# An attention and MLP kernel on one core: a new order of the same instructions, four stores for eight, and 64 products of zeros

## The chip, the cores and the metric

The kernel runs on one core of one Trainium2 chip. The metric is the device time of one execution in microseconds (us); the time of a kernel is the median of its runs. The engines are TensorE (PE, with PEld for its weight loads), VectorE (DVE), ScalarE (ACT), GpSimd (POOL) and SyncE (SP), which issues nearly all DMA.

## The reference

```python
kv = np.einsum('bhsd,bhse->bhde', k, v)            # 8 batches, 8 heads, 576 tokens, 64 wide
out = np.einsum('bhsd,bhde->bhse', q, kv)
out = out / np.sqrt(np.mean(out * out, axis=-1, keepdims=True) + 1e-6) * g_norm
x = out.transpose(0, 2, 1, 3).reshape(4608, 512)
h = x @ w_in                                       # 512 x 2048
return ((h * np.cos(h)) @ w_out).astype(np.float32)   # 2048 x 512
```

The weights arrive as 64-bit floats; everything is held to float32 accuracy.

## The kernel before

**Accuracy.** TensorE multiplies in a reduced float format (fp32r), so each operand is split into a high part and a low rest (`xhi`/`xlo`, `ghi`/`glo`, and the two halves of a weight tile), and each product is three: high by high, low by high, high by low. An operand costs a copy on ACT (the high part) and a subtraction on DVE or POOL (the rest).

**Chunks and steps.** The 4608 tokens are 9 chunks of 512. Chunks 0, 1 and 2 are worked plainly: a step is one tile of 128 hidden columns, `stage1_part` (12 products of 128x512 into a `bank`), `act_part` (h·cos h on ACT and DVE) and `stage2_part` (12 products into the four `acc` banks). The order is chunk 0 with tiles 0 to 3, chunk 1 with tiles 0 to 7, chunk 0 with 4 to 15, chunk 1 with 8 to 15, chunk 2. Between its two stretches chunk 0's sums are stored aside (`part0_0` to `part0_3`), and loaded again into a `slot` tile when they are completed (`out_part`). Chunks 3 to 8 are worked two at a time by a scheme with seven products in place of eight (`quad_part`), which needs sums and differences of w_in's tiles. `sums_part` makes them on POOL and stores them in DRAM (`wq`), from where they come back (`load_in`).

**The front.** Until the first step can run, k, v and q of the first two batches are loaded, `kv_front_part` and `x_front_part` make x for chunks 0 and 1, and `w_part` turns each raw weight tile into float32 and its two halves: on DVE a `TENSOR_SCALAR` on the low words (or the same on ACT), two `SCALAR_TENSOR_TENSOR` and one `TENSOR_TENSOR`, which writes the low half. 32 weight tiles pass through it in the first 130 us. The tiles are named `wi0` to `wi15` (w_in) and `wo0` to `wo15` (w_out); `m`, `sg`, `slot`, `r`, `ki` are shared working tiles.

**What sets the order.** Every engine works through its own queue in program order. That order is fixed when the kernel is built, by a planner in the kernel itself, class `Order`: each part asks for an engine and a time ("run"), waits for events or takes a token of a pool of buffers, and the planner hands the engines out by planned start and priority. The priorities are due times (`due`) plus a number for each part from the table `haste` (`put_off`); `gate` moves a part's earliest start by the same table. A DMA is planned as a time on SP, a time on the DMA engines and a delay until it counts as landed:

```python
    DMA_LAT = 1.6
    ...
    def flight(us, done):
        _, end = yield "run", [("DMA", us)], -1e3
        sched.give(t_fly, end + DMA_LAT)
        sched.fire(done, end + DMA_LAT)
```

The numbers decide nothing but the order: on the chip each instruction starts when its inputs and buffers are there. At the very start 40 products of zeros of 128x128 run on TensorE before the first data are in.

Of the kernel before, what the change touches and what calls it, by code (L numbers as in the profile page):

```python
# [10 lines left out]
F32 = mybir.dt.float32  # L11
# [174 lines left out]
def tile_kernel(  # L186
# [133 lines left out]
    def due(i):  # L320
# [7 lines left out]
        ('acc', 0): -308.36, ('acc', 1): 50.25, ('acc', 10): -89.24, ('acc', 11): -14.97, ('acc', 12): 244.72,  # L328
        ('acc', 13): -313.02, ('acc', 14): 115.67, ('acc', 15): -2.01, ('acc', 16): 9.58, ('acc', 17): -346.93,
        ('acc', 18): -115.97, ('acc', 19): 1122.67, ('acc', 2): 3.24, ('acc', 20): 388.25, ('acc', 21): 12.32,  # L330
        ('acc', 22): 45.65, ('acc', 23): 116.02, ('acc', 24): 93.39, ('acc', 25): -81.12, ('acc', 26): 284.61,
        ('acc', 27): 173.19, ('acc', 28): 102.47, ('acc', 29): 272.34, ('acc', 3): 49.44, ('acc', 30): -435.3,
        ('acc', 31): -431.32, ('acc', 32): -992.81, ('acc', 33): 118.14, ('acc', 34): 910.79,
        ('acc', 35): -309.89, ('acc', 36): 59.17, ('acc', 37): -20.74, ('acc', 38): -32.87, ('acc', 39): -11.87,
        ('acc', 4): -30.22, ('acc', 40): 329.51, ('acc', 41): 625.48, ('acc', 42): 79.92, ('acc', 43): 86.88,
        ('acc', 44): -161.65, ('acc', 45): 53.41, ('acc', 46): -145.28, ('acc', 47): 11.24, ('acc', 5): 244.28,
        ('acc', 7): 38.42, ('acc', 8): -20.95, ('acc', 9): -331.3, ('act', 0): -1.32, ('act', 1): -0.36,
        ('act', 10): 47.7, ('act', 11): -521.03, ('act', 12): -6.85, ('act', 13): -404.2, ('act', 14): -28.25,
        ('act', 15): -476.92, ('act', 16): 108.57, ('act', 17): -5.46, ('act', 18): -111.25, ('act', 19): 31.06,
        ('act', 2): 111.53, ('act', 20): 273.1, ('act', 21): -100.42, ('act', 22): -27.84, ('act', 23): -116.33,  # L340
        ('act', 24): -81.98, ('act', 25): -7.56, ('act', 26): -5.19, ('act', 27): -29.04, ('act', 28): 65.34,
        ('act', 29): -38.82, ('act', 3): 0.76, ('act', 30): -52.43, ('act', 31): 380.56, ('act', 32): 70.27,
        ('act', 34): -48.89, ('act', 35): 445.1, ('act', 36): -27.7, ('act', 37): -6.52, ('act', 38): 103.18,
        ('act', 39): -38.48, ('act', 4): -60.27, ('act', 40): 1650.37, ('act', 41): 104.72, ('act', 42): 179.73,
        ('act', 43): -0.49, ('act', 44): -9.15, ('act', 45): 28.81, ('act', 46): -152.26, ('act', 5): -0.59,
        ('act', 6): 50.53, ('act', 7): -7.88, ('act', 8): -0.49, ('act', 9): -221.89, ('cross', 0, 1): 14.87,
        ('cross', 1, 0): 270.69, ('cross', 1, 1): 237.31, ('cross', 2, 0): -223.42, ('cross', 2, 1): -397.6,
        ('gate keep in', 0): -313.88, ('gate keep in', 1): 77.44, ('gate keep in', 10): -411.52,
        ('gate keep in', 11): 38.86, ('gate keep in', 12): -993.27, ('gate keep in', 13): -979.61,
        ('gate keep in', 14): -141.94, ('gate keep in', 15): -16.43, ('gate keep in', 3): -727.27,  # L350
        ('gate keep in', 4): -1000.22, ('gate keep in', 5): 0.65, ('gate keep in', 6): -937.07,
        ('gate keep in', 7): 0.69, ('gate keep in', 8): 3.68, ('gate keep in', 9): -4.83,
        ('gate keep out', 0): 64.24, ('gate keep out', 1): 94.89, ('gate keep out', 10): -7.93,
        ('gate keep out', 11): -813.7, ('gate keep out', 12): -28.32, ('gate keep out', 13): -310.7,
        ('gate keep out', 14): -193.87, ('gate keep out', 15): -131.44, ('gate keep out', 2): 1.29,
        ('gate keep out', 3): 7.99, ('gate keep out', 5): -25.65, ('gate keep out', 6): -76.31,
        ('gate keep out', 7): 11.3, ('gate keep out', 8): 6.07, ('gate keep out', 9): 14.4,
        ('gate kv', 2): -119.99, ('gate kv', 3): 8.42, ('gate kv', 4): -89.12, ('gate kv', 5): -201.39,
        ('gate kv', 7): -260.05, ('gate load', 2): -1.73, ('gate load', 3): -19.79, ('gate load', 4): -246.31,
        ('gate load', 5): 23.96, ('gate load', 6): 1.63, ('gate load', 7): -70.84, ('gate sums', 0): -0.29,  # L360
        ('gate sums', 1): -1.99, ('gate sums', 2): 99.41, ('gate sums', 3): -10.12, ('gate sums', 4): -10.76,
        ('gate sums', 5): -175.34, ('gate sums', 6): 18.29, ('gate sums', 7): -6.45, ('gate x', 2, 0): -118.84,
# [153 lines left out]
    kv_tiles, q_tiles, xs, w_raw, w_split = {}, {}, {}, {}, {}  # L516


    DMA_LAT = 1.6

    t_fly = Tokens(8)

# [17 lines left out]
    def copies(out, in_, us):  # L540
        return us, lambda: sp.dma_start(out=out, in_=in_)
# [1191 lines left out]
```

## Time and profile before

| | |
|---|---|
| median of 3 runs | 843.74 us (841.93 to 843.87) |
| the profiled execution's own time | 844.5 us |
| its span, first to last instruction | 842.6 us |
| PE busy | 823.7 us, 98% of the span |
| DVE busy | 614.8 us, 73% |
| ACT busy | 501.8 us, 60% |
| POOL busy | 233.1 us, 28% |
| mean granted TensorE clock | 0.996 of full speed |

The busy time of PE holds its waits only where they are longer than the tail of the product before; its idle time is what is left of the span. A busy share over the whole span says little of the first 125 us, in which DVE is as full as PE.

### The profile page before, as it was taken

Reading aid. Unit: us, or ns where it says so; the run is one execution under the profiler, and the core shown is the slowest. Engines: PE = TensorE matmul, PEld = TensorE weight load, DVE = VectorE, ACT = ScalarE, POOL = GpSimd, SP = SyncE. Lnnn points to the kernel's source line nnn. Section 1 sums busy time; section 2 is a strip of 40 time slices with the busy share of each in tenths; the row PEclk is TensorE's granted clock in tenths of the full one; section 3 lists DMA queues with packets and bytes.
Section 4 is the critical chain, followed back from the end, with each engine's and each line's share of the span. In section 5 each row is a group of like instructions: output and inputs, shape, how many; then the busy total and the mean of one; then the engine's idle time right before and its main releaser. Section 6 shows DMA issues by size and latency. Waiting matters only on the chain.

```text
span 842.6 us, 12666 instructions
## 1 busy us (share of the span) xinstructions
PE 823.7 (98%) x4376; PEld 679.6 (81%) x4376; DVE 614.8 (73%) x949; ACT 501.8 (60%) x984; POOL 233.1 (28%) x154
## 2 busy tenths in 40 slices
PE   7899999999999999999999999999999999999998
PEld 6678878887888788887888888888888888888886
DVE  2999996566778888879889988898666774535221
ACT  4888964544455567768658756676555653535321
POOL 3220067542326783104226512305214000000000
PEclk9899999999999999999999999999999999999999
DMA  9997526698463588897966776677757676663664
GB/s 310 302 387 288 181 70 222 202 288 263 120 195 100 134 261 251 229 321 204 287 201 197 219 208 202 186 217 234 201 182 244 179 212 205 202 226 100 226 205 144
DMA packets 150912, 181.21 MB, mean 215 GB/s; under 512 B 74432, under 2 KB 114112, under 8 KB 150848
## 3 DMA queue, kind: packets, MB, share of 16 engines
q1 hardware_dynamic: 150336, 179.68, 69.3%
q8 instruction: 35, 0.57, 0.3%
q10 hardware_dynamic: 512, 0.72, 0.2%
q14 instruction: 29, 0.24, 0.1%
HBM read 143.66 MB, written 36.70 MB: 214 GB/s over the span
## 4 chain that ended last, share of the span: by engine, by line
PE 83%; DVE 7%; DMA 4%; ACT 2%; issue 2%; SPq 1%; POOL 0%; DVEq 0%; ACTq 0%; POOLq 0%
PE acc L239 43%; PE bank L239 40%; DVE sg L239 2%; SPq L239 1%; DVE r L239 1%; DMA wi<-in_moe_w_in_dram 1%; DVE wi L239 1%; DMA sg<-in_v_dram 1%; DMA wi<-in_q_dram 1%; DVE glo L239 0%; DVE xlo L239 0%; DVE slot L239 0%; DMA qb<-in_q_dram 0%; DMA out_dram<-slot 0%; DVE qT L239 0%
## 5 line engine op out<-in xcount | busy, mean ns | idle before, releaser
L239 PE MATMUL acc<-wo,ghi 128*128 128x512 f32 x1152 | 356.6, 390 | 0.9 <-DVE slot L239 0.6
L239 PEld LDWEIGHTS acc<-wo,ghi 128*128 128x128 f32 x1152 | 214.9, 188 | 46.3 <-DVE slot L239 1.3
L239 PE MATMUL bank<-wi,wo 128*128 128x512 f32 (+2 forms) x1092 | 241.5, 379 | 1.2 <-DVE wi L239 1.0
L239 PEld LDWEIGHTS bank<-wi,wo 128*128 128x128 f32 (+2 forms) x1092 | 191.3, 185 | 42.5 <-DVE wi L239 2.5
L239 PE MATMUL acc<-wo,glo 128*128 128x512 f32 x576 | 224.4, 390 | 0.0
L239 POOL TENSOR_TENSOR rinv<-ms,mhalf 128x16 f32<-128x16 f32 (+1 forms) x36 | 97.2, 2701 | 206.4 <-DVE ms L239 206.3
L239 PEld LDWEIGHTS acc<-wo,glo 128*128 128x128 f32 x576 | 108.1, 188 | 22.6
L239 PE MATMUL bank<-xhi,wi 128*128 128x512 f32 x320 | 99.9, 393 | 1.4 <-DVE slot L239 1.1
L239 DVE TENSOR_TENSOR wi<-bank,wi 128x512 f32<-128x512 f32 x72 | 49.5, 688 | 44.1 <-PE bank L239 35.4
L239 DVE TENSOR_TENSOR glo<-wo,ghi 128x512 fp32r<-128x512 f32 x59 | 42.8, 726 | 42.6 <-ACT ghi L239 42.4
L239 PEld LDWEIGHTS bank<-xhi,wi 128*128 128x128 f32 x320 | 59.2, 188 | 14.3 <-issue 1.5
L239 ACT ACTIVATE ki<-wi 128x512 int32<-128x512 f32 x72 | 45.1, 627 | 37.2 <-DVE wi L239 28.8
L239 ACT CAST ghi<-wo 128x512 fp32r<-128x512 f32 x61 | 37.8, 620 | 46.4 <-PE acc L239 45.8
L239 ACT ACTIVATE ki<-bank 128x512 int32<-128x512 f32 x72 | 42.7, 593 | 34.2 <-PE bank L239 29.0
L239 PE MATMUL bank<-xlo,wi 128*128 128x512 f32 x160 | 62.4, 390 | 0.0
L239 ACT COPY wi<-bank 128x512 f32<-128x512 f32 x72 | 41.9, 584 | 30.7 <-PE bank L239 30.0
L239 DVE TENSOR_TENSOR glo<-r,ghi 128x512 fp32r<-128x512 f32 x60 | 46.5, 777 | 11.5 <-ACT ghi L239 10.9
L239 ACT ACTIVATE r<-r 128x512 f32<-128x512 f32 x60 | 37.9, 631 | 22.3 <-DVE r L239 22.0
L239 DVE SCALAR_TENSOR_TENSOR r<-bank,ki 128x512 f32<-128x512 f32 x51 | 34.9, 685 | 21.8 <-ACT ki L239 21.6
L239 ACT ACTIVATE wo<-wo 128x512 f32<-128x512 f32 x61 | 38.2, 629 | 21.3 <-DVE wo L239 20.9
L239 ACT CAST ghi<-r 128x512 fp32r<-128x512 f32 x60 | 37.2, 621 | 22.3 <-PE acc L239 16.9
L239 DVE TENSOR_TENSOR r<-r,bank 128x512 f32<-128x512 f32 x51 | 34.7, 681 | 4.6 <-ACT r L239 3.9
(171 smaller groups left out, 1074.9 us busy)
## 6 DMA issues: line engine op xcount, KB each, us to landing
wo<-wod SPq DMA_DIRECT2D x96, 512.0 KB, 4.1
wo<-wq SPq DMA_DIRECT2D x84, 512.0 KB, 4.2
out_dram<-slot SPq DMA_DIRECT2D x35, 256.0 KB, 3.7
wi<-in_moe_w_in_dram SPq DMA_DIRECT2D x16, 512.0 KB, 8.9
wo<-in_moe_w_out_dram SPq DMA_DIRECT2D x16, 512.0 KB, 9.4
wod<-wo SPq DMA_DIRECT2D x16, 512.0 KB, 4.7
wq<-wi SPq DMA_DIRECT2D x24, 256.0 KB, 3.6
m<-in_k_dram SPq DMA_DIRECT2D x24, 256.0 KB, 4.8
```

What stands on the lines that cost most here:

```text
L239: return lambda *a, **kw: tc.keep_in_program_order(f(*a, **kw))
```

## The change

1. The table `haste` is replaced as a whole, and with it the order on every engine.
2. The planner's costs change: 0.5 for 0.4 us of SP for each DMA, a landing delay of 1.3 us for loads and 0.7 for stores in place of 1.6 for both, and other times for some DMAs and ACT copies.
3. `sums_part` makes the differences in another order and into another tile, so that two results that lie in regular steps in `wq` stand side by side. Each is stored by one DMA of 256 KB where two of 128 KB stood: 4 stores for 8 in each of 8 calls, 32 DMAs fewer in all.
4. A new part, `warm_part(16)`, gives TensorE 16 times 4 products of zeros of 128x128, into the bank of `acc2`, at the lowest priority, after x of chunk 0's first part is done.

```diff
-    DMA_LAT = 1.6
+    DMA_LAT, STORE_LAT = 1.3, 0.7
...
-            yield "run", [("SP", 0.4)], prio
+            yield "run", [("SP", 0.5)], prio
...
+    def warm_part(n):
+
+        yield "wait", [x_done[0, 0]]
+        yield "take", t_acc[2], 1e6
+        spare = ps_o.tile([P, DM], F32, name="acc2")
+        for _ in range(n):
+            _, end = yield "run", [("PE", 0.22)], 1e6
+            for _ in range(4):
+                pe.matmul(out=spare[:, 0:P], lhsT=zeros, rhs=zeros, start=True, stop=True)
+        sched.give(t_acc[2], end)
...
-        for t, places in ((even, (S1, A22)), (odd, (S3, S2))):
-            slot = yield "take", t_slot, prio
+        for t, places in ((rest, (S2, S3)), (even, (S1, A22))):
+            slot = spare if t is rest else (yield "take", t_slot, prio)
...
             sched.spawn(sums_store(slot, [stored], prio + 20.0, [
-                copies(wq[:, 7 * m + q, n], part[:, half * WH:(half + 1) * WH], 0.35)
-                for half, q in enumerate(places) for n, part in enumerate((hi.bitcast(F32), t))]))
+                stores(
+                    wq[:, first:last + 1:last - first, n, :], part.rearrange("p (h f) -> p h f", h=2), 0.68)
+                for n, part in enumerate((hi.bitcast(F32), t))]))
...
-        ('acc', 0): -308.36, ('acc', 1): 50.25, ('acc', 10): -89.24, ('acc', 11): -14.97, ('acc', 12): 244.72,
+        ('acc', 0): -572.9, ('acc', 1): 26.2, ('acc', 10): 92.3, ('acc', 11): -57.9, ('acc', 12): 191.2,
```

What the new table does shows in the order of the built programs. Counted over the whole program each engine has nearly the same instructions as before: PE 64 products more (the zeros), DVE 6 small copies more and 6 additions fewer, POOL 6 additions more, SP 32 DMAs fewer.

**TensorE in the front.** The place is that of chunk 0's x: `acc<-ident,r` turns x of one part back (a part's last product), `bank<-...64x64` is a `kv_front_part`. Before:

```order
L239 MATMUL bank_362<-wo_173,wi_172 64x64 x12
L239 MATMUL bank_383<-wo_171,wi_170 64x64 x18
L239 MATMUL acc_339<-ident,r_420 128x128 x4
L239 MATMUL acc_448<-wo_158,m_263 128x2x64 x4
L239 MATMUL bank_461<-ident,wi_174 128x128 x4
L239 MATMUL acc_352<-ident,r_467 128x128 x4
```

And with the change:

```order
L239 MATMUL bank_353<-wo_173,wi_172 64x64 x12
L239 MATMUL acc_240<-ident,r_301 128x128 x4
L239 MATMUL bank_388<-wo_171,wi_170 64x64 x18
L239 MATMUL bank_425<-ident,wi_174 128x128 x4
L239 MATMUL acc_330<-ident,r_414 128x128 x4
L239 LDWEIGHTS zeros
L239 MATMUL acc_424<-zeros 128x128
```

Twelve products of zeros follow here in a row; the other 52 stand in blocks of 4 to 24 between the front's products from here to the last x of chunk 0, and none behind that.

**VectorE ahead of w_out's tile 7.** The rows end with the one that writes the low half of `wo7`, which is the first operand of chunk 0's or 1's step 7 in stage 2. `sg`, `m` belong to `w_part`, `r`, `ki` and `bank` to `act_part`. Before:

```order
L239 TENSOR_TENSOR wo12_1493<-sg1_1396,wo12_1493 128x512
L239 TENSOR_TENSOR r1_1491<-r1_1491,bank3_1449 128x512
L239 TENSOR_SCALAR m1_1511<-wo15_864 128x512
L239 SCALAR_TENSOR_TENSOR sg2_1434<-wo7_332,sg2_1434 128x512
L239 SCALAR_TENSOR_TENSOR sg1_1509<-sg1_1509,m1_1511 128x512
L239 TENSOR_TENSOR wo7_1522<-sg2_1434,wo7_1522 128x512
```

And with the change:

```order
L239 TENSOR_TENSOR wo9_1579<-sg0_1487,wo9_1579 128x512
L239 SCALAR_TENSOR_TENSOR sg4_1539<-sg4_1539,m4_1556 128x512
L239 TENSOR_TENSOR r2_1585<-r2_1585,bank2_1535 128x512
L239 SCALAR_TENSOR_TENSOR r0_1611<-bank3_1566,ki_1603 128x512
L239 SCALAR_TENSOR_TENSOR sg4_1539<-wo7_323,sg4_1539 128x512
L239 TENSOR_TENSOR r0_1611<-r0_1611,bank3_1566 128x512
L239 TENSOR_TENSOR wo7_1624<-sg4_1539,wo7_1624 128x512
```

From DVE's first weight instruction (the `TENSOR_SCALAR` on the first weight tile's low words) to this row there were 172 instructions and are 180 (7 more of 128x512 with two tensors, 1 more `TENSOR_SCALAR` of 128x512). PE's first product with `wo7` had 345 products of 128x512 ahead of it and has 357. To the last `r<-bank,rinv` of chunk 1's x the same counts are 78 and 70 on DVE (7 and 1 fewer) and 90 and 69 on PE.

**SyncE where chunk 0's sums come back.** `slot<-part` loads the four sums again, `out_dram<-slot` stores the completed rows, `qb` loads q for chunk 2, `wod` and `wq` are stores of weights. Before:

```order
L239 DMA slot_2226<-part_1_1321_1045 128x512
L239 DMA qb_2183<-in_q_dram 32x4x32
L239 DMA slot_2229<-part_2_1359_1073 128x512
L239 DMA out_dram<-slot_2161 128x512
L239 DMA wod_142<-wo_739 128x1024
L239 DMA sg_2217<-in_v_dram 128x2x256
L239 DMA wq<-slot_2148 128x256
L239 DMA qb_2183<-in_q_dram 32x12x32
L239 DMA wod_152<-wo_1277 128x1024
L239 DMA wq<-sg_2015 128x256
```

The first sum's load stands 12 rows above these, the fourth's 5 rows below. With the change:

```order
L239 DMA slot_2191<-part_0_1341_1120 128x512
L239 DMA qb_2180<-in_q_dram 32x4x32
L239 DMA slot_2199<-part_1_1355_1128 128x512
L239 DMA qb_2180<-in_q_dram 32x12x32
L239 DMA qb_2222<-in_q_dram 32x4x32
L239 DMA qb_2180<-in_q_dram 32x12x32
L239 DMA qb_2222<-in_q_dram 32x4x32
L239 DMA qb_2180<-in_q_dram 32x12x32
L239 DMA qb_2222<-in_q_dram 32x4x32
L239 DMA qb_2180<-in_q_dram 32x12x32
```

The third sum's load comes 2 rows further on, the fourth's 6: the four stand within 16 rows, where they stood within 27, and no store of weights is between them.

## Rows read from the trace of the kernel before

**Rows 1.** The page: its first line of busy times (us, share, instructions), and of the 40 slices (21 us each) the rows of PE, DVE and the granted clock, in tenths.

```profile
PE 823.7 (98%) x4376; PEld 679.6 (81%) x4376; DVE 614.8 (73%) x949; ACT 501.8 (60%) x984; POOL 233.1 (28%) x154
...
PE   7899999999999999999999999999999999999998
...
DVE  2999996566778888879889988898666774535221
...
PEclk9899999999999999999999999999999999999999
```

**Rows 2.** Busy time in stretches: from:to, length, busy us and instructions of PE, PEld, DVE, ACT and POOL, then the granted clock, the DMA engines' share and GB/s.

```profile
18.00:24.00 6.00, 3.38 (x68) 2.65 (x67) 5.41 (x12) 4.98 (x13) 3.28 (x2) 1.00 1.09 355
24.00:31.00 7.00, 6.08 (x46) 5.11 (x48) 6.02 (x11) 4.87 (x11) 1.64 (x1) 0.52 1.11 259
...
60.00:110.00 50.00, 49.38 (x222) 40.97 (x223) 49.85 (x85) 44.38 (x81) 2.21 (x2) 1.00 0.64 226
110.00:123.00 13.00, 12.70 (x57) 10.21 (x56) 12.85 (x18) 6.38 (x12) 11.39 (x6) 1.00 0.27 81
...
180.00:205.00 25.00, 22.81 (x103) 18.19 (x102) 16.68 (x26) 10.41 (x21) 5.58 (x3) 1.00 0.89 253
205.00:400.00 195.00, 193.12 (x1081) 159.67 (x1080) 164.37 (x255) 122.39 (x256) 80.94 (x51) 1.00 0.71 203
400.00:839.00 439.00, 438.71 (x2076) 362.39 (x2074) 294.03 (x446) 246.22 (x468) 80.13 (x42) 1.00 0.66 203
```

**Rows 3.** The timeline of PE in the front: start, length, engine, line, operation, output and inputs, count, and in brackets the idle time before it and what ended it.

```profile
0.98 3.75 PE L239 MATMUL bank<-zeros 128*128 128x128 bf16 x40 [0.98 <-DVE zeros L239]
...
22.29 0.63 PE L239 MATMUL acc<-ident,r 128*128 128x128 f32 x4 [2.03 <-DVE r L239]
23.19 0.49 PE L239 MATMUL acc<-wo,m 128*128 128x128 f32 x2 [0.28 <-ACT wo L239]
24.92 1.65 PE L239 MATMUL acc<-wo,m 128*128 128x128 f32 x6 [1.24 <-ACT wo L239]
```

**Rows 4.** Single microseconds of the same kind as rows 2, where the granted clock falls and where it is back.

```profile
24.00:25.00 1.00, 0.08 (x1) 0.08 (x1) 1.00 (x2) 0.94 (x4) 0.00 (x0) 0.66 1.10 266
...
30.00:31.00 1.00, 1.00 (x15) 0.78 (x15) 1.00 (x2) 0.52 (x2) 0.22 (x1) 0.50 1.18 259
31.00:32.00 1.00, 0.84 (x20) 0.70 (x17) 1.00 (x3) 0.97 (x4) 0.00 (x0) 0.93 1.07 368
```

**Rows 5.** The timeline of DVE and PE: DVE's first weight instruction, its two waits while PE ran at half clock, the last `r` of chunk 1's x and PE's product behind it.

```profile
18.88 0.43 DVE L239 TENSOR_SCALAR m<-wi 128x512 int32<-128x512 uint32 x1 [0.20 <-DMA wi<-in_moe_w_in_dram]
...
27.24 0.69 DVE L239 TENSOR_REDUCE ms<-slot 128x8 f32<-128x512 f32 x1 [0.81 <-ACT slot L239]
...
32.78 0.69 DVE L239 TENSOR_TENSOR wi<-sg,wi 128x512 fp32r<-128x512 f32 x1 [0.45 <-ACT wi L239]
...
62.94 0.68 DVE L239 TENSOR_TENSOR r<-bank,rinv 128x512 f32<-128x512 f32 x1
...
63.87 0.60 PE L239 MATMUL bank<-ident,r 128*128 128x128 f32 x4
```

**Rows 6.** The timeline of POOL, DVE and PE around `wo7`: POOL's first sum, DVE's instructions beside it, and PE's wait.

```profile
109.74 5.51 POOL L239 TENSOR_TENSOR m<-wi 128x512 f32<-128x512 f32 x1 [47.10 <-DVE sg L239]
...
115.57 1.67 DVE L239 SCALAR_TENSOR_TENSOR sg<-wo,sg 128x512 int32<-128x512 int32 x1
...
119.80 1.22 DVE L239 SCALAR_TENSOR_TENSOR sg<-wo,sg 128x512 int32<-128x512 int32 x1
120.95 1.23 DVE L239 SCALAR_TENSOR_TENSOR sg<-sg,m 128x512 int32<-128x512 int32 x1
122.10 0.68 DVE L239 TENSOR_TENSOR wo<-sg,wo 128x512 fp32r<-128x512 f32 x1
...
122.83 0.50 PE L239 MATMUL acc<-wo,ghi 128*128 128x512 f32 x1 [0.30 <-DVE wo L239]
```

**Rows 7.** The timeline of SP's queue (SPq), DVE and PE where chunk 0's sums come back.

```profile
193.04 0.38 SPq L239 DMA_DIRECT2D slot<-part  x1
...
193.96 0.46 SPq L239 DMA_DIRECT2D slot<-part  x1
...
197.32 0.69 DVE L239 SCALAR_TENSOR_TENSOR slot<-acc,slot 128x512 f32<-128x512 f32 x1 [3.21 <-DMA out_dram<-slot]
...
198.07 0.73 PE L239 MATMUL acc<-wo,ghi 128*128 128x512 f32 x2 [0.59 <-DVE slot L239]
...
201.01 0.70 PE L239 MATMUL bank<-xhi,wi 128*128 128x512 f32 x2 [1.13 <-DVE slot L239]
```

**Rows 8.** PE's other waits between 123 and 400 us: what waited for what, us in total, times, the longest.

```profile
PE bank L239 <- DVE wi L239: 1.0, 1, 1.0
...
PE bank L239 <- DVE r L239: 0.5, 1, 0.5
PE bank L239 <- DVE sg L239: 0.5, 1, 0.5
```

**Rows 9.** The timeline of DVE: the instructions ahead of the first and the last of these waits.

```profile
182.91 1.79 DVE L239 TENSOR_TENSOR sg<-qT,m 128x512 fp32r<-128x512 f32 x1
...
389.42 1.75 DVE L239 SCALAR_TENSOR_TENSOR xhi<-wi,ki 128x512 f32<-128x512 f32 x1
```

**Rows 10.** The page's DMA issues: what was moved by which queue, how often, KB each, median us to landing.

```profile
wq<-slot SPq DMA_DIRECT2D x32, 128.0 KB, 2.6
...
wq<-sg SPq DMA_DIRECT2D x16, 128.0 KB, 2.8
```

**Rows 11.** A stretch in which PE does nothing but products of 128x512, columns as in rows 2.

```profile
600.00:700.00 100.00, 100.00 (x443) 82.76 (x442) 69.85 (x101) 57.29 (x104) 13.18 (x8) 1.00 0.66 204
```

More of the change, by code (lines that the diff above doesn't have):

```diff
@@ L333, in tile_kernel @@
[L333 to L337, printed above, removed]
@@ L354, in tile_kernel @@
[L354 to L359, printed above, removed]
@@ L516, in tile_kernel, with flight, copies, stores @@
     kv_tiles, q_tiles, xs, w_raw, w_split = {}, {}, {}, {}, {}
-    DMA_LAT = 1.6
+    DMA_LAT, STORE_LAT = 1.3, 0.7
     t_fly = Tokens(8)
-    def flight(us, done):
+    def flight(us, late, done):
         _, end = yield "run", [("DMA", us)], -1e3
-        sched.give(t_fly, end + DMA_LAT)
-        sched.fire(done, end + DMA_LAT)
+        sched.give(t_fly, end + late)
+        sched.fire(done, end + late)
     def dmas(pieces, prio):
         landed = []
-        for us, issue in pieces:
+        for us, late, issue in pieces:
             yield "take", t_fly, prio
-            yield "run", [("SP", 0.4)], prio
+            yield "run", [("SP", 0.5)], prio
             issue()
             landed.append(Event())
-            sched.spawn(flight(us, landed[-1]))
+            sched.spawn(flight(us, late, landed[-1]))
         yield "wait", landed
         return max(e.t for e in landed)
-    def copies(out, in_, us):
-        return us, lambda: sp.dma_start(out=out, in_=in_)
+    def copies(out, in_, us, late=DMA_LAT):
+        return us, late, lambda: sp.dma_start(out=out, in_=in_)
+    def stores(out, in_, us):
+        return copies(out, in_, us, STORE_LAT)
     def load(prio, event, pieces, wait=(), take=None, first=None):
@@ L655, in pieces @@
                 src = moe_w_out[j * P:(j + 1) * P, :].rearrange("p (c f) -> p c f", f=P)
-            return [copies(t, src, 1.4 if kind == "wi" else 1.3)]
+            return [copies(t, src, 1.5 if kind == "wi" else 1.4)]
         return pieces
@@ L696, in copies @@
         def copies(j):
-            e, end = yield "run", [("ACT", 0.3, 0.0), ("DVE", 0.3, 0.3)], prio
+            e, end = yield "run", [("ACT", 0.45, 0.0), ("DVE", 0.45, 0.3)], prio
             for r in heads:
@@ L984, in x_norm @@
         sched.give(t_qT, end)
-        yield "run", [("ACT", 0.6)], prio
+        yield "run", [("ACT", 0.87)], prio
         swp = small.tile([P, TB], F32, name="swp")
@@ L1006, in x_norm @@
             aside = tc.dram_tile([P, CH], F32, name=f"x{c}_{p}")
-            end = yield from dmas([copies(aside, x, 0.68)], prio)
+            end = yield from dmas([stores(aside, x, 0.66)], prio)
             sched.give(t_slot, end, held)
@@ L1010, in x_norm @@
             x = store_tile(held)
-            end = yield from dmas([copies(x, aside, 0.68)], due(begin[PLAIN - 1]) + p)
+            end = yield from dmas([copies(x, aside, 0.9)], due(begin[PLAIN - 1]) + p)
         if c >= PLAIN:
@@ L1225, in out_part @@
         if before is not None:
-            yield from dmas([copies(o, before, 0.68)], prio)
+            yield from dmas([copies(o, before, 0.85)], prio)
             _, end = yield "run", [("DVE", dve_us(DM))], prio
@@ L1238, in out_part @@
             to = partial[c, t] = tc.dram_tile([P, DM], F32, name=f"part{c}_{t}_{sched.seq}")
-        end = yield from dmas([copies(to, o, 0.68)], prio)
+        end = yield from dmas([stores(to, o, 0.68)], prio)
         sched.give(t_slot, end, slot)
@@ L1281, in keep_in @@
         end = yield from dmas([
-            copies(wq[:, 7 * m + q], w[:, :, half * WH:(half + 1) * WH].bitcast(F32), 0.68)
+            stores(wq[:, 7 * m + q], w[:, :, half * WH:(half + 1) * WH].bitcast(F32), 0.68)
             for q, half in (((A11, 0), (A12, 1)) if j % 2 == 0 else ((S4, 1),))], prio)
@@ L1287, in keep_out @@
         yield "wait", [w_done["wo", j]]
-        end = yield from dmas([copies(wod[j], w_split["wo", j].bitcast(F32), 1.3)], prio)
+        end = yield from dmas([stores(wod[j], w_split["wo", j].bitcast(F32), 1.3)], prio)
         sched.fire(wo_kept[j], end)
@@ L1310, in sums_part @@
         pool.tensor_tensor(out=even, in0=odd, in1=even, op=ALU.subtract)
-        for out, a, b in (
-            (odd[:, low], odd[:, high], odd[:, low]),
-            (odd[:, high], odd[:, high], even[:, low]),
-            (even[:, high], even[:, low], even[:, high]),
-        ):
+        yield "run", [("POOL*", pool_us(WH))], prio
+        pool.tensor_tensor(out=even[:, high], in0=even[:, low], in1=even[:, high], op=ALU.subtract)
+        spare = yield "take", t_slot, prio
+        rest = slot_tile(spare)
+        for out, a, b in ((rest[:, low], odd[:, high], even[:, low]), (rest[:, high], odd[:, high], odd[:, low])):
             yield "run", [("POOL*", pool_us(WH))], prio
@@ L1318, in sums_part @@
         kept = []
-        for t, places in ((even, (S1, A22)), (odd, (S3, S2))):
-            slot = yield "take", t_slot, prio
+        for t, places in ((rest, (S2, S3)), (even, (S1, A22))):
+            slot = spare if t is rest else (yield "take", t_slot, prio)
             yield "run", [("ACT", act_us())], prio
-            hi = at.tile([P, CH], F32R, name=f"slot{slot}", bufs=1)
+            if t is rest:
+                hi = two(pair, [P, CH], F32R, 1)
+            else:
+                hi = at.tile([P, CH], F32R, name=f"slot{slot}", bufs=1)
             act.copy(out=hi, in_=t)
```

181 lines of the change are left out of this document (94 added, 87 removed), and 90 rows, old and new, of the table haste.

## The prediction

> **What bounds the kernel now.** I read the page's busy shares first. PE is busy 98% of the span, and 9 tenths or more in nearly every slice [rows 1]; the products themselves stay what they are, so only PE's waits and its slow stretch can be won. Next the stretches [rows 2]: behind 400 us PE has 0.3 us of idle time in 439, so nothing is to be had there, and the 3.7 us between the last product and the end of the span are the last stores. What is left lies in three places.
>
> First the front. From 18 us on DVE is as full as PE: 49.85 of 50 us between 60 and 110, 85 instructions, so 0.59 us from one to the next. PE has no such queue of its own making: it waits for `r`, the `wi` and the `wo` that DVE writes. The last such wait is 0.30 us, at 122.83 us, for the low half of `wo7`, which DVE wrote from 122.10 to 122.78 [rows 6]. So up to 123 us the end is set by DVE's queue: when DVE reaches `wo7`, and how much of PE's work is done by then. Second the clock: it falls to 0.5, the lower of its two levels (1.2 GHz), in the microsecond after 24 and is back in the one after 31 [rows 4]. Before it fell PE had waited 2.03, 0.28 and 1.24 us with little between [rows 3]. From 24.92 to 31 PE is busy at half speed, so it does about 3 us less than it could. But that is worth on the path only what DVE loses by it: DVE waits 0.81 and 0.45 us there for ACT's copies of what PE delivers late [rows 5]. Third five waits between 123 and 400 us: 0.59 and 1.13 us where chunk 0's sums come back [rows 7], and 1.0, 0.5 and 0.5 us elsewhere [rows 8].
>
> **The change, part by part.**
>
> *The zeros.* 64 more products. The 40 at the start take 3.75 us, 0.094 each [rows 3], so 64 cost PE 6.0 us at most, and nothing where they fill a wait. They stand among the products of 20 to 35 us, where PE waits for DVE and where 2.03 and 1.24 us of waits were; behind the last x of chunk 0 there are none. I charge nothing on the path, because DVE's queue sets the end there; if PE were the later one, the cost would be up to 6.0 less the waits that they fill. What they can give is the clock. If it holds, DVE's two waits shrink: −0.9 us of the 1.26, bounds 0 and −1.3. The Trainium skill, page "TensorE: Matmul & The Clock Gate", section "HAM oscillation — how this bites in real kernels", says that it is the long idle gaps between bursts that send the array back to half clock; the trace agrees in kind, but here the longest gap was 2.03 us. By that rule a filler that leaves such gaps changes nothing, and the −0.9 would be 0.
>
> *DVE's queue to `wo7`.* From the first weight instruction (18.88 us [rows 5]) to `wo7` there were 172 instructions and are 180. Seven more with two tensors at 0.59 and one short one at about 0.35 (its 0.43 less the overlap): +4.5 us. The start: the first weight tile is now the 13th of SP's loads and was the 14th; one load of v of 0.29 MB less at 355 GB/s [rows 2] is −0.8 us (0 to −0.9). The waits of DVE: −0.9, from above. POOL: its first sum starts at 109.74, and DVE's instructions beside it take 1.67, 1.22 and 1.23 us in place of the 0.68 of `wo7`'s own row [rows 6], 2.1 us more together; and DVE's 18 instructions from 110 to 123 us fill 12.85 us [rows 2], where 18 at 0.59 fill 10.6: about 2.2 us are lost beside POOL. In the new order POOL's first sum writes a tile that DVE reads last 12 rows ahead of `wo7`, and five of these 12 read or write PSUM banks, which DVE also had among the rows here without being slowed. Before, the sum began some 17 rows ahead. I take −0.9; bounds −2.2 (all of it gone) and +4.7 (each of the seven others takes 1.67: 6.9 us, less the 2.2 that are lost now). So `wo7` comes 4.5 − 0.8 − 0.9 − 0.9 = 1.9 us later. But PE has 12 more products of 128x512 behind it by then, at 100 us for 443 [rows 11] 0.226 each, 2.7 us. The front is worth 1.9 − 2.7 = **−0.8 us**, and from −2.6 (all bounds at their best) to +6.5 (neither start nor waits won, and the 4.7).
>
> The same sum for the last `r` of chunk 1's x (62.94 us [rows 5]): 8 instructions fewer, −4.5, the start −0.8, the waits −0.9, and 21 products fewer done, +4.7: −1.5. That gives PE more than `wo7` lets it keep, so `wo7` decides.
>
> *Chunk 0's sums.* The loads that end the waits are issued at 193.04 and 193.96 [rows 7], behind stores of weights and loads of q on SP; DVE stands 3.21 us and then adds at 197.32, and PE waits 0.59 and 1.13 us for the banks. In the new order two loads stand ahead of most of q's, and the fourth 13 rows nearer to the first. Each row that SP has less ahead of it is about 0.4 us. That should take most of the 1.72 us: **−1.3** (0 to −1.7).
>
> *The other waits.* Of the 2.0 us [rows 8] two follow DVE instructions of 1.79 and 1.75 us [rows 9], more than twice their usual time, both in stretches in which POOL works. The trace of before can't say whether the new order sets such a pair again; the same engines do the same work. I take **−0.6**, from −2.0 (none comes back) to +2.0 (as much again is added).
>
> *Four stores for eight.* 32 DMAs less on SP, each about 0.4 us of SP, 128 KB with 2.6 to 2.8 us to landing [rows 10]; 256 KB take longer each. No wait of PE ends with one of them: 0 on its own; its share in SP's queue is in the term above. The sums take as many instructions on POOL as before.
>
> *The sum.* −0.8 − 1.3 − 0.6 = −2.7 us against the profiled execution's own 844.5, 841.8 us. That execution is 0.8 above the median of the runs shown, so the median to expect is **841.0 us**.
>
> **The rivals.**
>
> *No change that can be told* (within 0.3%, 2.5 us, which is about what a measurement of this kernel can tell from none). The waits come back elsewhere: with the last two terms at 0, only the front's −0.8 stays, 843.0 us. For it: PE idles only 4.0 us between 123 and 839, so little is there to win, and DVE is full in both orders. Against it: the loads of the sums have plainly moved.
>
> *The fillers don't hold the clock.* They run as soon as PE comes to them, so a wait for DVE or a DMA behind a block is only shortened by it, not filled. Then DVE's 0.9 isn't won and PE is again at half clock for some 7 us: 841.9 us, and if the slow stretch falls where stage 1 has begun, where PE has no slack, up to 3 us more. Against it: PE had next to nothing between its three waits, and now has blocks of 4 to 24 products there.
>
> *Slower.* DVE and POOL meet in the 12 rows ahead of `wo7`. If each of the seven rows there with both inputs in SBUF takes the 1.67 us of the worst row in rows 6, that is 4.7 us more than now in place of 0.9 less, the front is +4.8, and with half of the other two terms the time is 847.6 us; with none of them 848.5. It decides from a `wo7` at about 125.5 us on: later than that, each us is one at the end. The Trainium skill, page "SBUF — State Buffer", section "SBUF: two separate sides", says that the port pair of VectorE and GpSimd is an exclusive lock for a whole instruction. Rows 6 and 9 agree that single instructions grow by about 1 us, and that not all of them do. Against it: the planner sets the same pair of engines in both orders, and POOL's first sum begins nearer to `wo7` than it did.
>
> **How the numbers follow.** My forecast, faster, holds 48%: its own range is 838 to 841.2. No change, by either of the first two rivals, 38%; slower 14%. All bounds at their best give 844.5 − 2.6 − 1.7 − 2.0 − 0.8 = 837.4; I start the range at 837.5, and end it at 845.5, inside the no-change case, beyond which the slower one and a part of the second rival lie, together under 2 in 10.
>
> **What would show it right or wrong.** The granted clock stays at 1.0 from 20 to 35 us, or falls again. DVE's first weight instruction is at about 18.1 us. `wo7` is written at about 124.7 us, with PE waiting under half a microsecond; with more than 126 the front lost. The waits `acc<-` and `bank<-DVE slot` near 200 us are gone or under 0.5 us together. PE's idle time between 123 and 400 us is under 3 us. The prediction is wrong if DVE has longer waits of its own in the front, for weights that land later in the new order of loads, or if a new wait of over 1 us stands where chunks change.

## The result, and the profile after

The changed kernel takes 849.65 us (median of 9 runs, 847.13 to 856.37), the kernel before 842.96 us beside it: a ratio of 1.0085, 95% interval 1.0058 to 1.0112. It is slower by 0.6 to 1.1%, and outside the range that was given. The profiled execution took 849.77 us, its span is 848.0. The three runs with a mean granted clock of 1.00 took 847.1 to 847.6 us, the six at 0.991 to 0.998 took 849.1 to 856.4. The first line of the page, as in [rows 1]:

```profile
PE 827.5 (98%) x4440; PEld 681.5 (80%) x4440; DVE 610.6 (72%) x951; ACT 500.6 (59%) x976; POOL 241.5 (28%) x160
```

TensorE's busy share is the same, and tells nothing: it holds the zeros, and products at half clock.

The stretches of [rows 2], in the kernel after, with the same columns (from:to, length, busy us and instructions of PE, PEld, DVE, ACT and POOL, granted clock, DMA share, GB/s):

```profile
18.00:24.00 6.00, 4.97 (x83) 4.11 (x78) 5.72 (x12) 5.68 (x15) 3.74 (x2) 1.00 1.10 324
24.00:31.00 7.00, 5.89 (x98) 5.25 (x98) 6.90 (x14) 5.81 (x15) 2.20 (x2) 1.00 1.11 308
...
60.00:110.00 50.00, 50.00 (x222) 41.41 (x221) 49.62 (x86) 43.19 (x78) 0.00 (x0) 1.00 0.56 200
110.00:123.00 13.00, 13.00 (x59) 10.76 (x58) 12.84 (x21) 11.07 (x21) 4.65 (x3) 1.00 0.76 261
...
180.00:205.00 25.00, 24.96 (x116) 20.72 (x115) 21.27 (x36) 13.85 (x31) 5.81 (x2) 1.00 0.66 179
205.00:300.00 95.00, 93.86 (x569) 77.76 (x568) 68.34 (x115) 47.40 (x106) 58.63 (x38) 1.00 0.55 157
300.00:400.00 100.00, 94.99 (x479) 76.96 (x479) 77.07 (x115) 63.03 (x121) 23.09 (x19) 0.98 0.80 252
400.00:839.00 439.00, 436.75 (x2066) 359.55 (x2065) 302.31 (x456) 252.83 (x482) 96.97 (x50) 1.00 0.68 208
```

Up to 205 us everything is better than before: the granted clock stays at 1.00 (0.52 in [rows 2] from 24 to 31 us), TensorE is never idle between 60 and 123 us, and from 180 to 205 us it lacks 0.04 us where it lacked 2.19. The loss lies behind 300 us: 5.0 us of idle time to 400 us and 2.25 behind it, where the kernel before has 1.2 and 0.3 (behind 400 us in [rows 2]; its line for 300 to 400 us follows):

```profile
300.00:400.00 100.00, 98.79 (x512) 81.47 (x511) 87.06 (x132) 71.48 (x140) 31.58 (x24) 1.00 0.86 255
```

Then the two traces are laid side by side product by product, without the zeros, each shape of product at the pace that it has in the trace of before. By this TensorE after is ahead by 1.7 us when the kernel before is at 117 us, by 4.4 us at 300, by 0.9 at 346; it is behind by 3.3 at 365, by 1.5 at 407 and by 5.4 from 560 us to the end. So a lead of 4.4 us is lost and 5.4 more: 9.8 us, of which 7.7 between 300 and 365 and 3.9 behind 407, with 1.8 won back between, where the kernel before has waits of its own.

Where it goes is told by TensorE's waits there, as in [rows 3] (start, length, operation, and in brackets the idle time before it and what ended it):

```profile
307.83 1.63 PE L239 MATMUL bank<-wi,wo 128*128 128x512 f32 x6 [1.21 <-DMA wo<-wq]
...
327.00 0.73 PE L239 MATMUL bank<-wi,wo 128*128 128x512 f32 x2 [0.51 <-ACT wi L239]
...
328.76 0.50 PE L239 MATMUL bank<-wi,wo 128*128 128x512 f32 x1 [1.03 <-DVE wi L239]
...
361.96 4.58 PE L239 MATMUL bank<-wi,wo 128*128 128x512 f32 x12 [2.19 <-DMA wo<-wq]
...
432.22 1.66 PE L239 MATMUL bank<-wi,wo 128*128 128x512 f32 x6 [0.84 <-ACT wi L239]
...
460.52 0.50 PE L239 MATMUL bank<-sg,kv_w 128*128 128x384 f32 x2 [0.55 <-DVE r L239]
```

Behind the wait of 2.19 us the clock falls to its lower level, so 12 products take 4.58 us and not the 2.7 that 12 times 0.226 makes. The four waits up to here (4.9 us) and this 1.9 are 6.8 of the 7.7 us; where the rest is lost these rows don't tell. Single microseconds of that stretch:

```profile
362.00:363.00 1.00, 1.00 (x4) 0.78 (x5) 0.44 (x1) 0.00 (x0) 0.00 (x0) 0.72 1.03 421
363.00:364.00 1.00, 1.00 (x4) 0.81 (x3) 0.00 (x0) 0.00 (x0) 0.00 (x0) 0.50 1.04 426
```

The chain that ended last shows what is late (start, length, what; `SPq` is SyncE's queue). It is the same pattern three times: a transfer on which SyncE stands, or behind which it issues, and then the load that TensorE waits for:

```profile
298.38 5.13 DMA x<-slot
...
303.57 0.32 SPq L239
...
303.98 3.72 DMA wo<-wq
...
307.83 3.01 PE bank L239 x12
...
316.74 4.96 DMA x<-slot
...
321.76 3.82 DMA wo<-x
...
327.02 1.70 DVE wi L239
...
348.59 6.49 DMA m<-in_k_dram
...
355.46 6.36 DMA wo<-wq
```

`x<-slot` stores a quarter of chunk 4's x (256 KB) aside in DRAM, `wo<-x` loads it back, `wo<-wq` loads a w_in tile for chunks 3 and 4. SyncE's queue at the third place:

```profile
347.56 0.32 SPq L239 DMA_DIRECT2D wo<-wq  x1
347.93 0.61 SPq L239 DMA_DIRECT2D k_over<-in_k_dram  x1
348.59 2.70 SPq L239 DMA_DIRECT2D m<-in_k_dram  x4
351.35 0.61 SPq L239 DMA_DIRECT2D v_over<-in_v_dram  x1
352.00 2.85 SPq L239 DMA_DIRECT2D sg<-in_v_dram  x3
355.46 0.34 SPq L239 DMA_DIRECT2D wo<-wq  x1
```

Nine loads of k and v stand ahead of the w_in tile that TensorE wants at 359.8 us. The buffer for it was free at 352.3, when the twelfth of the 42 products that start at 349.41 was done (in the first experiment below the load waits for nothing but that product). It is issued at 355.46, while loads of k and v are still on their way, and takes 6.36 us, where the page's median for these loads is 4.3.

### The profile page after: what moved, and what is told of

It reads as the page before. It is cut to its first block, busy times and chain, and to the rows that moved or that the text cites. A ratio compares the mean times of both kernels' runs of the same rounds, so it can differ in the third digit from the quotient of the medians.

```text
span 848.0 us, 12779 instructions
## 1 busy us (share of the span) xinstructions
PE 827.5 (98%) x4440; PEld 681.5 (80%) x4440; DVE 610.6 (72%) x951; ACT 500.6 (59%) x976; POOL 241.5 (28%) x160
## 4 chain that ended last, share of the span: by engine, by line
PE 74%; DMA 11%; DVE 8%; ACT 3%; issue 2%; POOL 1%; SPq 1%; DVEq 0%; ACTq 0%
PE acc L239 38%; PE bank L239 36%; DMA wi<-in_moe_w_in_dram 2%; DVE r L239 2%; DMA x<-slot 1%; POOL rinv L239 1%; DMA wo<-wq 1%; DMA wo<-in_v_dram 1%; DVE glo L239 1%; DVE slot L239 1%; DVE xlo L239 1%; DMA m<-in_k_dram 1%; DMA wi<-in_k_dram 1%; DVE qT L239 1%; DVE wo L239 1%
## 5 line engine op out<-in xcount | busy, mean ns | idle before, releaser
L239 PE MATMUL bank<-wi,wo 128*128 128x512 f32 (+2 forms) x1092 | 246.0, 380 | 8.0 <-DMA wo<-wq 3.4
```

What stands on the lines that cost most here:

```text
L239: return lambda *a, **kw: tc.keep_in_program_order(f(*a, **kw))
```

## The experiments

Theory A: the time is lost where loads stand late in SyncE's queue, and nowhere else on the way. Rival B: TensorE comes 4 us earlier than in the kernel before to a place where nothing is ready any sooner, so the lead is lost whatever SyncE issues first. To tell them apart SyncE's DMAs are counted as they are issued, and single ones are held back until a later one is out; the queues of all other engines stay as changed, row by row.

### Three loads of v behind the w_in tile

```diff
+    HOLD = {332: 335, 333: 335, 334: 335}
+    held_back, turn = {}, [0]
+
+    def in_turn(issue):
+        n = turn[0]
+        turn[0] += 1
+        if n in HOLD:
+            held_back.setdefault(HOLD[n], []).append(issue)
+            return
+        issue()
+        for late in held_back.pop(n, ()):
+            late()
...
-            issue()
+            in_turn(issue)
```

> The changed kernel with one row of SyncE's queue moved: the load of the w_in tile that TensorE waited for at 361.96 us (2.19 us, and half clock behind it) is issued ahead of three loads of v and not behind them. Theory A (the time is lost where loads stand late in SyncE's queue): that load is issued at about 352 and not 355.4 us, the 2.19 us shrink to under 0.5, and no run has a granted clock under 0.999; the median is 845.5 to 847 us in place of 849.65. Rival B (TensorE comes 4 us earlier to this place than in the kernel before, and whatever it needs next isn't there either): it then waits at about 365 us for k and v, 1.5 us or more, and the median stays at 848 to 850.

Measured: 847.63 us, ratio 1.0040 (1.0012 to 1.0067). The wait is 0.45 us and the 12 products behind it run at the full clock, in 3.00 us:

```profile
360.57 3.00 PE L239 MATMUL bank<-wi,wo 128*128 128x512 f32 x12 [0.45 <-DMA wo<-wq]
```

No wait for k and v takes its place, against B. The load is issued at 352.68 us. The time is at the end 0.6 us above what A expected, and the mean clock was under A's 0.999 in four of the six runs, so half clock comes in other places too: in the profiled run (0.998) for 3.4 us from 13.1 us on.

### The x stores and reloads ahead of loads that have time

```diff
-    HOLD = {332: 335, 333: 335, 334: 335}
+    HOLD = {298: 299, 303: 309, 306: 309, 308: 309}
```

> The changed kernel with four loads moved in SyncE's queue: the first w_in tile for chunks 3 and 4 goes ahead of the reload of chunk 4's x, whose store SyncE stood for 4.31 us, and two w_in loads and one of w_out go behind the last x's store and reload. Theory A: TensorE's waits of 1.21 us at 307.83 and of 0.51 and 1.03 us near 328 go to under 0.6 together, 2 to 2.7 us less, 847 us at the median, with the wait at 362 us still there. Rival B: a later wait grows by as much, 849 to 850 us.

Measured: 846.69 us, ratio 1.0033 (1.0014 to 1.0053). None of the three waits at 308 to 329 us is left in the trace, as A has it (0.31 us stand at 337 us); the third place is left, with 1.70 us:

```profile
359.15 2.96 PE L239 MATMUL bank<-wi,wo 128*128 128x512 f32 x12 [1.70 <-DMA wo<-wq]
```

### Both moves

> Both moves together, seven rows of SyncE's queue, all else as in the changed kernel. Theory A: the two gains add up, 4.5 to 6.5 us, 843 to 845 us, as fast as the kernel before or within 0.3% of it, and the granted clock is 1.0 in all runs. Rival B: 847 us or more, since the lead of 4.4 us that TensorE has at 300 us can't be kept whatever stands first on SyncE.

Measured: 842.86 us (841.07 to 845.94), ratio 0.9995 (0.9976 to 1.0015). Seven moved rows of one queue give back 6.8 us, as much as the change had lost. TensorE has no wait at all between 300 and 365 us; its lead over the kernel before is 2.9 us at 300 and 2.8 at 365. What is left stands further on, and the longest of it is the one that the changed kernel has at 432 us:

```profile
426.46 1.66 PE L239 MATMUL bank<-wi,wo 128*128 128x512 f32 x6 [0.84 <-ACT wi L239]
```

B falls: the lead is kept when SyncE issues in another order. Two parts of A fall too. The granted clock is 0.996 to 1.00 and not 1.0 in all runs, and the time isn't lost in these places alone: behind 407 us this trace loses 4.2 us of lead, as the changed kernel does.

### No zeros in the front's gaps

```diff
-            for _ in range(4):
-                pe.matmul(out=spare[:, 0:P], lhsT=zeros, rhs=zeros, start=True, stop=True)
+            pass
```

> The changed kernel in the same order on every engine, without the 64 products of zeros. What the prediction held (the zeros keep the clock): without them the granted clock falls to 0.5 between 20 and 32 us again, and TensorE's lead over the kernel before at 123 us is 1 us or more smaller than the 1.7 us of the changed kernel. At the end: theory A and B both say that the waits at 308 to 362 us take it up, 848.5 to 850.5. Rival C (the zeros themselves, 5.6 us of TensorE, are what made it slower): 845 to 847.

Measured: 846.62 us, ratio 1.0034 (1.0016 to 1.0052). The clock falls at 29 us, as expected:

```profile
29.00:30.00 1.00, 0.43 (x8) 0.46 (x10) 1.00 (x4) 0.94 (x4) 1.00 (x1) 0.58 1.13 412
30.00:31.00 1.00, 1.00 (x22) 0.93 (x18) 1.00 (x2) 0.62 (x2) 1.00 (x2) 0.50 1.05 415
31.00:32.00 1.00, 0.84 (x7) 0.71 (x4) 1.00 (x3) 0.94 (x5) 1.00 (x1) 0.50 1.06 340
```

But TensorE's lead isn't smaller by 1 us: it is at the same product at 117 us 0.3 us *earlier* than with the zeros. In this trace half clock costs DVE nothing: from 29.2 to 36 us it is busy 6.56 of the 6.8 us, and 6.33 with the zeros. And the end came 3 us sooner than with zeros, which A and B didn't have; rival C, the time of the zeros themselves, did, and is put to the test from here on.

### The changed kernel again, and both moves without zeros

> The changed kernel itself once more, so that the edits of this call have it beside them on the same chip. 847 to 851 us at the median; TensorE waits for the w_in load near 362 us (over 1.5 us) and once or more near 308 to 329 us in the profiled execution.

Measured: 850.11 us, ratio 1.0067 (1.0051 to 1.0083), with the waits of 0.31, 0.40, 1.03 and 2.85 us at the same four places.

> The seven moved rows of SyncE and no zeros. The run without zeros was 3 us below the changed kernel's median, though on another chip and with TensorE at 123 us no later than with them. Theory D (the zeros cost nothing and give nothing at the end, DVE's queue sets it): the same as with both moves and zeros, 842 to 843.5 us. Rival E (without zeros the runs are faster by what they showed): 840 to 841 us.

Measured: 844.16 us, ratio 1.0001 (0.9981 to 1.0022). The time is 0.7 us above D's range and 3 above E's. With the moved rows the zeros make no difference that these runs can tell, so E falls, and that the run without zeros was faster points to the late loads.

### Eight stores again

```diff
-                stores(
-                    wq[:, first:last + 1:last - first, n, :], part.rearrange("p (h f) -> p h f", h=2), 0.68)
+                halves(wq, places, m, n, part)
...
+    def halves(wq, places, m, n, part):
+        def issue():
+            for half, q in enumerate(places):
+                sp.dma_start(out=wq[:, 7 * m + q, n], in_=part[:, half * WH:(half + 1) * WH])
+        return 0.68, STORE_LAT, issue
```

> The changed kernel in the same order, with each of the 32 stores of 256 KB of w_in's sums issued as two of 128 KB as in the kernel before; the sums themselves stay as changed. The prediction put nothing on the stores by themselves: the same as the changed kernel beside it within 1.5 us. Rival F (the larger stores sit in the way of loads, so that these land late): the w_in loads near 304 and 352 us land sooner, and the time falls by 2 us or more. 32 more DMAs of about 0.4 us on SyncE speak the other way, for up to 1 us more.

Measured: 848.41 us, ratio 1.0058 (1.0040 to 1.0077). That is 1.7 us less than the changed kernel beside it, but the intervals overlap, and the late loads are there as before: the large stores aren't what makes them late (rival F). Whether they cost or give a microsecond these runs don't tell.

```profile
310.20 1.63 PE L239 MATMUL bank<-wi,wo 128*128 128x512 f32 x6 [1.37 <-DMA wo<-wq]
...
365.00 4.41 PE L239 MATMUL bank<-wi,wo 128*128 128x512 f32 x12 [3.19 <-DMA wo<-wq]
```

### Where TensorE's instructions come in

The store of x at 298.38 us took 5.13 us, its like without zeros 2.6. From 298 to 301 us the DMA engines are full, and then for two microseconds hardly anything moves, while the store isn't done (columns as in rows 2; the last two are the share of the 16 DMA engines and GB/s):

```profile
300.00:301.00 1.00, 1.00 (x8) 0.87 (x8) 0.88 (x3) 0.50 (x2) 0.92 (x2) 1.00 1.05 355
301.00:302.00 1.00, 1.00 (x6) 0.82 (x5) 1.00 (x1) 0.97 (x3) 0.97 (x1) 1.00 0.11 36
302.00:303.00 1.00, 1.00 (x6) 0.84 (x5) 0.97 (x3) 0.95 (x3) 0.74 (x1) 1.00 0.06 14
```

0.06 of 16 engines is one engine at work. It is the end of what was under way: from 301.4 to 302.1 us no packet starts, and from 302.2 to 303 six of 2 KB, one after the other. The page lists transfers of instructions, which no line of the kernel issues; between 300 and 302 us there is one of them, of 16 KB, and it lasts 1.96 us. On the page (queue, kind, packets, MB, share of 16 engines):

```profile
q8 instruction: 35, 0.57, 0.3%
```

And the same list for the two microseconds from 300 to 302:

```profile
q8 instruction: 1, 0.02, 6.1%
```

It ends at 302.1 us, just when these last packets begin, so they stood behind it on the same engine. 4440 products and as many weight loads in 35 transfers are some 250 instructions in each, so the transfers are TensorE's. In the changed kernel they start at 300.1, 322.7 and 357.4 us, on the three late chains; without the 64 zeros, which are 128 instructions, they stand half a transfer apart, at 279.2 and 306.9 us. Theory J: where these transfers fall decides how late a late load is. It is tested by shifting them and nothing else.

```diff
     for _ in range(40):
         pe.matmul(out=bank[:, 0:P], lhsT=zeros, rhs=zeros, start=True, stop=True)
+    for _ in range(64):
+        pe.matmul(out=bank[:, 0:8], lhsT=zeros, rhs=zeros[:, 0:8], start=True, stop=True)
```

> The changed kernel with 64 more products of zeros, 8 columns wide, behind the 40 at the very start, so that TensorE's program is 128 instructions longer ahead of everything else; all queues are otherwise as changed. TensorE's instructions come in by transfers of 16 KB, one for about every 250 of them, each on one of the 16 DMA engines for 1 to 2 us. In the changed kernel one starts at 300.1 us, in the middle of the store of x that SyncE waits for until 303.5; without the 64 zeros of the gaps they stood half a transfer apart from there, at 279 and 307. Theory J (where the instruction transfers fall decides how late the late loads are): here too they stand half a transfer apart from those of the changed kernel, near 282 and 310 us, the wait near 308 us goes, and the median is 845.5 to 848 us although the program does more. Rival K (the zeros in the gaps cost TensorE time): 850 us or more, since it has all of them and 64 more.

Measured: 847.48 us (843.34 to 853.59), ratio 1.0047 (1.0018 to 1.0077). The second kernel has these 64 too, but not those of the gaps:

> The changed kernel without the 64 products of zeros in the front's gaps, and with 64 of 8 columns behind the 40 at the very start: as many instructions as the changed kernel from there on. Theory J: the transfers of 16 KB stand where the changed kernel has them (one near 300 us), the store of x takes 4.5 us or more to land, the wait near 308 us is back, and the median is 848.5 to 851 us. Rival K: as fast as without the zeros or up to 1 us later for the start, 846 to 848 us.

Measured: 851.07 us (849.64 to 853.58), ratio 1.0100 (1.0075 to 1.0125). SyncE's queue, the store of x and the reload that stands on it, first without zeros, then with 64 more, then with 64 moved:

```profile
296.80 0.32 SPq L239 DMA_DIRECT2D x<-slot  x1
...
299.44 0.32 SPq L239 DMA_DIRECT2D wo<-x  x1
```

```profile
298.07 0.32 SPq L239 DMA_DIRECT2D x<-slot  x1
...
300.84 0.32 SPq L239 DMA_DIRECT2D wo<-x  x1
```

```profile
299.10 0.32 SPq L239 DMA_DIRECT2D x<-slot  x1
...
303.83 0.32 SPq L239 DMA_DIRECT2D wo<-x  x1
```

From store to reload it is 2.64, 2.77 and 4.73 us, with transfers of 16 KB at 279.2 and 306.9, at 280.2 and 307.9, and at 300.9 us. Of the four kernels the two whose transfers fall at 300 us take 849.7 and 851.1 us, the two with the other phase 846.6 and 847.5, wherever the zeros stand. The intervals of 846.6 (no zeros) and 851.1 (64 moved) don't overlap, so K falls: the second has no zeros in the gaps either. That of 847.5 (64 more) overlaps the changed kernel's, and there the trace carries the verdict: no wait at 308 us, but 2.57 us, and half clock behind it, at the third place, where the k and v loads stand in front in any phase.

So J holds for the store at 298 us. How the 4.5 us between those two kernels arise is shown in part only. In the profiled executions they are 5.7 us apart at the end: 1.2 of it stands at 117 us already, 1.1 comes up to 300 us, and 4.3 between 300 and 365. But the wait at 308 us is only 0.55 us with the 64 moved, and the waits near 328 us are 1.4 us in sum without zeros and 1.8 with 64 moved. Most of the 4.3 us is half clock for 3.4 us from 329.8 and again from 363.9 us, which at half speed costs 1.7 us each time, and which the other trace doesn't have there; that the phase of the transfers is behind that too is not shown.

### Table and costs apart

In the first of two runs the changed kernel is planned with the costs of before (`DMA_LAT, STORE_LAT = 1.6, 1.6`, 0.4 us of SyncE, the old times of DMAs and copies); in the second the new costs go with the table of before.

> The changed kernel's table, sums and zeros, planned with the old costs (1.6 us until a load or a store counts as landed, 0.4 us of SyncE a DMA, the old times of DMAs and copies). In the order that this gives, the first two w_in loads stand ahead of the reload of chunk 4's third x, but the nine loads of k and v still stand ahead of the w_in load that was late at 362 us. Theory G (the new costs put the loads behind the x stores, the new table put k and v late): no wait at 308 us, the one near 362 us of 1.5 us or more stays; 846.5 to 849 us. Rival H (table and costs only work as a pair): new waits elsewhere, over 850 us. Rival I (the costs did all of it): 844 us or less.

Measured: 872.71 us, ratio 1.0348 (1.0294 to 1.0402).

> The new costs, the new sums and the zeros with the old table. Theory G in part (the new table put k and v late): in this order the k and v loads of the first such group stand behind the first w_in load, near 305 us, as in the kernel before, so there is no wait near 362 us; but two reloads of x stand right behind their stores, so SyncE waits there by 2 us or more. With costs and table not made for each other a wait of several us elsewhere is likely, since the reverse pairing came to 872.7 us: 845 to 875, and no forecast nearer than that.

Measured: 897.52 us, ratio 1.0639 (1.0605 to 1.0673). Each has waits in the front that neither whole kernel has; the longest of the two runs:

```profile
83.46 0.80 PE L239 MATMUL acc<-wo,glo 128*128 128x512 f32 x1 [8.51 <-DVE glo L239]
```

```profile
85.47 2.24 PE L239 MATMUL bank<-wo,m 128*32 128x128 f32 x20 [16.02 <-ACT m L239]
```

G said 846.5 to 849 for the first and fell, H holds: a table is good for the costs that it was made with. In neither does TensorE wait more than 0.61 us for a w_in load; but it comes to these places late (the two end 23 and 48 us behind the changed kernel), so that this shows little of which part, table or costs, made the loads late.

### Both moves, a quarter of a transfer further

The seven moved rows and 32 of the products of 8 columns at the start.

> The changed kernel with the seven moved rows of SyncE and 32 more products of zeros of 8 columns at the very start, which shifts TensorE's instruction transfers by a quarter of their distance. The runs with the moved rows fell in two groups, five from 841.1 to 841.7 and five from 844 to 846. Theory J: another phase changes how many fall in each group; if it keeps the transfers clear of the x stores and w_in loads, 841 to 842 us at the median, under the kernel before by 0.2 to 0.3%; if it hits another load, 844 to 846.

Measured: 842.79 us (840.12 to 845.50), ratio 0.9996 (0.9981 to 1.0010): as fast as the kernel before. The median lies between the two ranges that J named, and the ten runs fall in no two groups, so this run says nothing for J. No variant with the changed order is faster than the kernel before by more than can be told.

## Why the prediction was wrong

**The front: right in size, as far as single traces tell.** Forecast −0.8 us. TensorE is 1.7 us ahead at 117 us in the profiled execution and 0.6 in the repeated one; in the four more with this front (the three runs with moved rows, the eight stores) it is 1.4, 1.0, 0.3 and −0.3. That is 0.8 in the mean, against one trace of the kernel before, so the match is no better than these differences. Of its terms: DVE's first weight instruction is at 17.89 us, 1.0 earlier (forecast 0.8), but at 18.3 to 20.2 us in the other five traces, so that term isn't shown. `wo7` is written from 122.61 us, and done by 123.6 where 124.7 was forecast (123.6 to 125.6 in the six), and TensorE has no wait for it:

```profile
115.60 1.50 DVE L239 TENSOR_TENSOR glo<-r,ghi 128x512 fp32r<-128x512 f32 x1
...
122.61 1.00 DVE L239 TENSOR_TENSOR wo<-sg,wo 128x512 fp32r<-128x512 f32 x1
```

Beside POOL these two grew, by 0.8 and 0.3 us, where the three of [rows 6] grew by 2.1: 1.0 less lost, the forecast's 0.9. So the rival that had DVE and POOL collide ahead of `wo7` did not come, though its sign did.

**The zeros: right on the clock, wrong on its worth.** In all eight traces with the 64 zeros in the gaps the clock is 1.00 from 20 to 36 us. Without them it is at half from 29 to 36 us in two of three; in the third, both moves without zeros, it had fallen for 3.4 us at 13.9 us and is 1.00 from 18 us on. So the second rival's condition, that fillers don't hold the clock, finds no support. The "−0.9 us of the 1.26" was to come from there. At half clock DVE is busy 6.56 of the 6.8 us without zeros and 5.72 with the 64 moved, against 6.33 with them in the gaps: what DVE gained came in the main from the order, and holding the clock is worth 0.6 us to it at most in these traces. The second of its two waits, which ended at 32.78 us, lies behind the half clock (back at 31.1) anyway. In full the zeros were costed as work in gaps; that 128 more instructions shift the instruction transfers for the other 800 us was not in the sum. Zeros put in or taken out moved the median by 2 to 4.5 us in this order, and by nothing that can be told with seven rows of SyncE moved.

**Chunk 0's sums: right, and more than forecast.** Forecast −1.3; the 2.19 us of idle time from 180 to 205 us are 0.04. The three traces with moved rows and zeros have one wait of 0.4 to 0.9 us there, at 194 or 195 us.

**The other waits: here the prediction failed.** Its term was "−0.6, from −2.0 (none comes back) to +2.0 (as much again is added)", for the waits from 123 to 400 us. What came was 7.7 us between 300 and 365, and 3.9 behind 407, where the prediction had no term at all: "nothing is to be had there" is right for gains, but an order can lose there too. TensorE idles 6.3 us from 123 to 400, where under 3 was named. (Before, by [rows 2], it idles 4.4 us between 123 and 839, not the 4.0 of the prediction; that changes nothing.) The bound was taken from the size of the old waits, as if a new order could only set such waits again. But the order was there to be read: a reload of x right behind its own store with a w_in load behind it, and nine loads of k and v in front of another. From each store of chunk 4's x to its reload the trace of before has 2.1 to 4.8 us, so the first place could be priced; the prediction looked behind 205 us for waits that DVE's long instructions make, and for no others. "A new wait of over 1 us where chunks change" was named as what would make it wrong; chunks 3 and 4 begin there.

The planner's new number, 0.7 us until a store has landed, is short of every store of x measured: 2.0 us to the reload at the least, in both kernels. It puts the reload early and so lets SyncE stand. That this is why the table came to this order is argued, not shown: the run with the old costs changed too much else.

**Four stores for eight: nothing, as forecast**, as far as 2 us can tell.

**Open.** The 3.9 us behind 407 us. By the same comparison all eleven traces with this order lose 3.0 to 4.4 us there, with zeros and without, in either phase, with SyncE's rows moved or not. From 400 us on DVE is busy 47.81 of 50 us up to 450 us against 42.82 before, ACT 39.94 against 33.49, and both end TensorE's waits. The wait of 0.83 or 0.84 us at 426 to 435 us stands in all eleven too, which fits work crowded on DVE and ACT by the order; no run took it apart.

## What to carry to other kernels

Where a queue works in program order, read the rows behind each transfer that waits for another transfer to land, and ask what the engine that is never idle needs from behind it; a store and its reload must stand a whole landing apart with loads that have time in between, not in front. A planner that counts a store as landed too soon will put them together. Bound a new order's waits by reading the order, not by the waits of the old one; and judge a small edit of a long program with its instruction transfers shifted once or twice, since 64 useless products of 8 columns moved the time by half a per cent here.

## What the runs showed of the hardware

TensorE's instructions come in by transfers of 16 KB on the kernel's own DMA engines, 35 in this run, each 0.9 to 2.0 us long on one engine. A store of 256 KB spread over all 16 lands when the slowest is done: the third of chunk 4's x took 2.6 to 2.8 us clear of such a transfer and 4.5 to 5.1 us across one, and the reload of the fourth 2.5 to 2.7 and 3.5 to 3.8. It isn't the only thing that makes a store late: the fourth itself, issued 0.4 to 0.8 us behind a w_in load of 512 KB, took 4.7 to 5.0 us in five traces with no such transfer across it, and 2.0 us to its reload where it was moved ahead of that load. The Trainium skill, page "Runtime: NRT & Kernel Launch", section "Instruction fetch mechanics", says that instructions are refilled in blocks of 16 KiB and that crossing a block's boundary costs one bump of a DMA queue, mostly hidden. The size agrees with the 16 KB of each transfer here; hidden it is for TensorE, which doesn't wait for its instructions at 300 us, but not for the data transfer that shares the engine.

A wait can cost nearly twice its length: behind the 2.19 us at 362 us the clock fell and 1.9 us more were lost. In the other runs the waits of 2.15, 2.57, 2.85 and 3.19 us at this place were followed by half clock too, those of 0.45, 1.70 and 1.94 us were not. The length of one wait doesn't settle it: with the 64 moved the clock also fell behind waits of 0.77 and 1.03 us near 328 us, and behind 0.51 and 1.03 us there in the changed kernel it didn't.
